# Two memory-attention and gMLP blocks: the gMLP rebuilt with tokens on partitions and started during the attention's last rows, attention weights kept on chip, the input read directly

## The chip, the cores and the metric

One core of one Trainium2 chip. The metric is the device time of one execution in microseconds (us). TensorE, its weight loads, VectorE, ScalarE, GpSimd and the issuing queue of SyncE are called PE, PEld, DVE, ACT, POOL and SP below, as in the profile.

## The reference

The input is one sequence of 2048 tokens with 512 features. Four residual steps follow each other: attention A, gMLP B, A again, B again, each on a layer norm of x, with the same weights in both rounds.

```python
x = x + A(layernorm(x));  x = x + B(layernorm(x))      # twice
# A: 64 segments of 32 tokens, one after the other; 32 heads of 128
h = concat([mem, xs])                  # 8 memory rows and 32 tokens
q, k, v = h @ Wq, h @ Wk, h @ Wv
o = softmax(mask(q @ k.T * scale)) @ v @ Wo
mem = o[:8];  out_segment = o[8:]
# B: 688 gate features
z = gelu(x @ w_in);  z1 = z[:, :688];  z2 = layernorm(z[:, 688:])
y = (z1 * (w_sp @ z2 + b_sp[:, None])) @ w_out         # w_sp: 2048 x 2048 over tokens
```

A is a chain: the memory of a segment is the output of the one before. B mixes all tokens, so its gate needs every tile of z2.

## The kernel before

**Start.** 12 MB of Wq, Wk, Wv and 4 MB of Wo are loaded on the queues of SP, ACT and POOL, in pieces of 1 MB. The input comes behind Wo on ACT's queue, 16 tiles of 128 tokens; each is cast to f32 in the permuted column order that A uses, written to the DRAM buffer `xd`, and its mean and variance are taken (`_stats`, L111 on, into `MV`). One Sqrt over all 16 tiles and a reciprocal (`_ln_scalars`, L104) then give the reciprocal deviation of every tile.

**A** (`a_block`). `ln_load` and `ln_apply` normalise a tile, write it to DRAM (`xn_d`) and read it back in two layouts (`preB`, `pre`). `b_units` projects the last eight rows of each segment of a tile (psb, L404). `segment` runs 64 times: projections of 32 rows (psm, L404), scores, softmax, values, `wo_pass` (pw, L495), which gives the next memory and so the next `hA` (L560). `spare` holds work for DVE's gaps. The output rows go to DRAM (`oA_d`, `oB_d`). `y_load` (L530 to 535) gathers a tile of them and of x with nine DMAs on SP, `y_add` adds them on DVE (L542), stores the tile to `xd` and takes its statistics. At the end come one last `wo_pass`, 32 matmuls for the last group of rows (pwB, L504), and then `y_load` and `y_add` for tile after tile through a single buffer, for the six tiles that are left.

**B** (`b_block`). First `_ln_scalars` over all 16 tiles, so every row of A must be done. Then every tile of x is loaded, normalised on DVE (L156), transposed on PE (pT, L160) and copied into `xnT` by ACT. z2 is projected with tokens on partitions (L168, L171), z1 with features on partitions (L183). The norm of z2 waits for the statistics of all tiles (L188), and then writes z2n, half the tiles on DVE (L191) and half on ACT (L194). `w_sp` comes through transposing DMAs of 256 tokens, 1 MB each, two buffers (L206); the pool of these buffers is opened when the first half is closed. The gate then has features on partitions: per 256 tokens 6 chunks of features (the last one 48 wide) by 16 token tiles of matmuls with 256 columns (pg, L223), the bias added on DVE (L226), the product with z1 on POOL (L227), and 12 matmuls with w_out (py, L234). In the first B, POOL issues the load of the attention weights for the second round at the start of this stage (`mid_hook`).

**Order.** In A, the order of PE, DVE and ACT is that of the code (`manual_schedule`); in B, the framework orders all engines. POOL and SP are ordered by the framework throughout. A queue issues its DMAs in order, and a DMA that waits holds up those behind it.

Of the kernel before, what the change touches and what calls it, by code (L numbers as in the profile page):

```python
# [26 lines left out]
FCH = [(0, 128), (128, 128), (256, 128), (384, 128), (512, 128), (640, 48)]  # L27

# [10 lines left out]
class _RR:  # L39

    def __init__(self, engines):
        self.engines = list(engines)
        self.i = 0

    def __call__(self):
        e = self.engines[self.i % len(self.engines)]
        self.i += 1
        return e


def _consts(ctx, tc):
    nc = tc.nc
    cp = ctx.enter_context(tc.tile_pool(name="consts", bufs=1))
    tctx = ExitStack()
# [42 lines left out]
    c["maskM"] = maskM  # L97
    c["MV"] = [cp.tile([P, 16, 2], F32, name=f"MV{i}") for i in range(2)]
    tctx.close()
# [4 lines left out]
def _ln_scalars(nc, pool, MV, NT, c):  # L104
    rstd = pool.tile([P, NT], F32, name="rstd")
    nc.scalar.activation(out=rstd[:], in_=MV[:, 0:NT, 1], func=ACT.Sqrt, bias=c["eps_t"][:], scale=1.0)  # L106
    nc.vector.reciprocal(out=rstd[:], in_=rstd[:])
    return MV[:, 0:NT, 0], rstd
# [8 lines left out]
def b_block(tc, c, xd, MV_in, MV_out, w_in, w_sp, b_sp, w_out, S, out_final=None, mid_hook=None):  # L117
    nc = tc.nc
    NT = S // P
    TCW = min(512, S)  # L120
    NTC = S // TCW
    TC2 = min(256, S)
    NTC2 = S // TC2
    with ExitStack() as ctx:
        mid = ctx.enter_context(tc.tile_pool(name="b_mid", bufs=1))
        ps_pool = ctx.enter_context(tc.tile_pool(name="b_ps", bufs=1, space=PSUM))
        ps = _Tagged(ps_pool, "acc", 6)
        pst = _Tagged(ps_pool, "tp", 2)
        z1T = mid.tile([P, 6, S], BF16, name="z1T")
        z2n = mid.tile([P, NT, FH], BF16, name="z2n")  # L130
        w_out_sb = mid.tile([P, 6, DM], BF16, name="w_out_sb")
        nc.scalar.dma_start(w_out_sb[:, 0:5, :], w_out[0:640, :].rearrange("(fc p) d -> p fc d", p=P))
        nc.scalar.dma_start(w_out_sb[0:48, 5, :], w_out[640:688, :])
        bsp_bc = mid.tile([P, S], BF16, name="bsp_bc")
        nc.gpsimd.dma_start(bsp_bc[:], b_sp.partition_broadcast(P))

        with ExitStack() as c1:
# [11 lines left out]
            for tt in range(NT):  # L149
                xs = xp.tile([P, DM], F32, name="xs")  # L150
                xq().dma_start(xs[:], xd[tt * P:(tt + 1) * P, :])
                xs_tiles.append(xs)
# [643 lines left out]
```

## Time and profile before

| | |
|---|---|
| median of 3 runs | 2098.46 us (2096.6 to 2102.81) |
| the profiled execution | 2104.0 us |
| its span, first to last instruction | 2102.3 us |
| busy in the span: PE, PEld, DVE, ACT, POOL | 85%, 51%, 59%, 49%, 7% |
| granted TensorE clock, mean | 0.958 |
| DMA | 144.79 MB, 69 GB/s over the span |

Matmuls are pipelined, so the time of one contains the way through the array: 96 matmuls that are called 273 ns each pass in 10.71 us. A pace is therefore read from starts, not from a mean. "Issue" is idle time for which the profile shows no wait. The view by stages gives, for stretches of the span, the busy time of each engine with the number of instructions in brackets, the granted clock and the DMA engines' busy share and rate.

### The profile page before, as it was taken

The numbers are of one execution on the slowest core, as the hardware profiler recorded it, in microseconds if no ns is written. First come the engines' busy times: TensorE is split into PE (matmuls) and PEld (weight loads), VectorE is DVE, ScalarE is ACT, GpSimd is POOL, SyncE is SP. The second block draws the span as 40 slices with busy tenths as digits, with TensorE's granted clock in tenths as the row PEclk, the third lists the DMA queues.
The fourth block names the chain that finished last, engine by engine and source line by source line (L and its number), as shares of the span: only waits on it lengthen the run. The fifth ranks groups of instructions, "written<-read, shape, count | busy, mean of one in ns | idle before, by whom it ended". The sixth has DMA issues, their size and how long they took to land.

```text
span 2102.3 us, 95923 instructions
## 1 busy us (share of the span) xinstructions
PE 1788.5 (85%) x44288; PEld 1076.1 (51%) x44288; DVE 1247.1 (59%) x2732; ACT 1024.3 (49%) x1798; POOL 138.6 (7%) x287
## 2 busy tenths in 40 slices
PE   0599999999999998273986999999999999973899
PEld 0255555555555554132753555555555555542476
DVE  1576766777777765241334676767867777644322
ACT  0366666656666664170003666656666666532500
POOL 2000000000000000001320000000000000000022
PEclk9999999999999999696998999999999999996999
DMA  9300001021002002528551000000200120044253
GB/s 355 118 24 19 21 19 27 23 68 37 20 26 79 20 15 85 168 63 253 146 172 54 23 19 27 24 20 26 79 20 20 41 71 18 10 129 130 51 141 91
DMA packets 172115, 144.79 MB, mean 69 GB/s; under 512 B 97088, under 2 KB 139712, under 8 KB 168640
## 3 DMA queue, kind: packets, MB, share of 16 engines
q1 hardware_dynamic: 146016, 83.76, 14.9%
q10 hardware_dynamic: 21728, 30.78, 4.2%
q0 software_dynamic: 3968, 24.12, 3.1%
q8 instruction: 346, 5.67, 1.1%
q14 instruction: 57, 0.47, 0.1%
HBM read 88.13 MB, written 33.70 MB: 58 GB/s over the span
## 4 chain that ended last, share of the span: by engine, by line
PE 66%; ACT 11%; DVE 9%; issue 7%; DMA 4%; SPq 1%; POOL 1%; ACTq 0%; DVEq 0%; POOLq 0%
PE psm L404 22%; PE pw L495 11%; PE psb L404 9%; PE pg L223 8%; DVE KA L588 4%; ACT rows L584 4%; ACT E L612 3%; PE psO L631 3%; PE pwB L504 3%; PE psS L608 3%; DVE E L615 2%; DMA xb<-in_A_x_dram 2%; PE psM L675 2%; PE psD L684 2%; PE py L234 1%
## 5 line engine op out<-in xcount | busy, mean ns | idle before, releaser
L404 PEld LDWEIGHTS <-hA 128*32 128x32 bf16 x12288 | 304.4, 96 | 309.1 <-DVE hA L560 54.2
L584 ACT CAST rows<-psm 128x512 bf16<-128x512 f32 x512 | 299.7, 585 | 187.4 <-PE psm L404 187.4
L495 PE MATMUL pw<-Wo_sb,uT 128*32 128x128 bf16 x16640 | 266.6, 219 | 30.5 <-issue 23.4
L404 PE MATMUL psm<-Wq_sb,hA 128*32 128x512 bf16 x4096 | 272.5, 381 | 11.7 <-DVE hA L560 11.6
L495 PEld LDWEIGHTS <-uT 128*32 128x32 bf16 x16640 | 245.2, 97 | 70.4 <-issue 31.9
L404 PE MATMUL psm<-Wk_sb,hA 128*32 128x512 bf16 x4096 | 268.5, 379 | 0.0
L404 PE MATMUL psv<-Wv_sb,hA 128*32 128x512 bf16 x4096 | 268.0, 382 | 0.0
L588 DVE STREAM_TRANSPOSE QQ<-rows 128x512 bf16<-128x512 bf16 x256 | 182.2, 712 | 81.2 <-ACT rows L584 80.7
L223 PE MATMUL pg<-wspT,z2n 128*128 128x256 bf16 (+1 forms) x1536 | 177.0, 277 | 57.1 <-issue 47.2
L647 DVE TENSOR_TENSOR uT<-psO,Rt 128x384 bf16<-128x384 f32 x256 | 138.0, 539 | 138.3 <-ACT Rt L637 138.3
L588 DVE STREAM_TRANSPOSE KA<-rows 128x512 bf16<-128x512 bf16 x256 | 182.0, 711 | 39.5 <-ACT rows L584 37.2
L223 PEld LDWEIGHTS <-z2n 128*128 128x128 bf16 (+1 forms) x1536 | 151.4, 100 | 82.5 <-issue 64.5
L612 ACT ACTIVATE E<-psS 128x448 bf16<-128x448 f32 x256 | 140.0, 547 | 107.5 <-PE psS L608 107.5
L594 DVE CAST VA<-psv 128x512 bf16<-128x512 f32 x256 | 175.4, 685 | 2.4
L226 DVE TENSOR_TENSOR gb<-pg,bsp_bc 128x256 f32<-128x256 f32 x96 | 40.6, 423 | 209.1 <-PE pg L223 209.1
L404 PEld LDWEIGHTS <-hB 128*32 128x32 bf16 x3072 | 75.4, 97 | 158.1 <-DVE hB L453 76.5
L404 PE MATMUL psb<-Wq_sb,hB 128*32 128x512 bf16 x1024 | 69.5, 393 | 100.5 <-DVE hB L453 76.5
L608 PEld LDWEIGHTS <-KA 128*64 128x64 bf16 x2048 | 79.8, 113 | 127.8 <-DVE KA L588 127.8
L553 POOL COPY QQ<-QTB 128x256 bf16<-128x256 bf16 x128 | 49.4, 401 | 1406.8 <-DVE QTB L483 795.6
L637 ACT ACTIVATE Rt<-Rt 128x1024 f32<-128x1024 f32 x128 | 135.3, 1057 | 4.1
L636 ACT ACTIVATE Rt<-psD 128x1024 f32<-128x1024 f32 x128 | 128.6, 1005 | 0.1
L106 ACT ACT_TABLE_LOAD x6 | 7.7, 1283 | 229.5 <-DMA Wo_sb<-in_A_Wo_dram 161.7
(97 smaller groups left out, 2377.5 us busy)
## 6 DMA issues: line engine op xcount, KB each, us to landing
xs<-xd SPq DMA_DIRECT2D x48, 256.0 KB
xs<-xd ACTq DMA_DIRECT2D x48, 256.0 KB
oA_d<-o_sb SPq DMA_DIRECT2D x130, 64.0 KB
xs_y<-xd SPq DMA_DIRECT2D x32, 256.0 KB
xd<-ot_y SPq DMA_DIRECT2D x32, 256.0 KB
Wq_sb<-in_A_Wq_dram POOLq DMA_DIRECT2D x6, 1024.0 KB, 16.7
Wk_sb<-in_A_Wk_dram POOLq DMA_DIRECT2D x6, 1024.0 KB, 25.0
Wv_sb<-in_A_Wv_dram POOLq DMA_DIRECT2D x6, 1024.0 KB, 20.6
```

The source lines that it names most:

```text
L223: nc.tensor.matmul(pg[0:fsz, :], lhsT=z2n[:, st_i, f0:f0 + fsz], rhs=wspT[:, st_i, :], start=(st_i == 0), stop=(st_i == NT - 1))
L404: nc.tensor.matmul(ps[32 * cg:32 * cg + 32, :], lhsT=lhs(kt, cg), rhs=rhs(kt, cg), start=(kt == 0), stop=(kt == KT - 1), tile_position=(0, ...
L495: nc.tensor.matmul(po[32 * cg:32 * cg + 32, 0:128], lhsT=lhs[:, n, :], rhs=wo_rhs(h, cg), start=(h == 0), stop=(h == H - 1), tile_position ...
L504: nc.tensor.matmul(pwB[:], lhsT=oBs[G][:, n, :], rhs=Wo_sb[:, h, :].rearrange("p (kt g el) -> p g kt el", kt=4, g=4), start=(h == heads[0] ...
L584: nc.scalar.copy(r[:], ps[:])
L588: nc.vector.transpose(out=QQ[:, j % 2, :, 0:32] if j < 2 else KA[:, j % 2], in_=r[:])
L594: nc.vector.tensor_copy(VA[:, r].rearrange("p i e -> p (i e)"), ps)
L608: nc.tensor.matmul(pS[64 * g:64 * g + 64, i, c0:80 if K is KA else 112], lhsT=K[:, r, n:n + 2, :].rearrange("p h k -> p (h k)"), rhs=q if ...
L612: nc.scalar.activation(out=E[:, r], in_=pS, func=ACT.Exp, scale=scale)
L636: nc.scalar.activation(out=o, in_=in_, func=ACT.Ln)
L637: nc.scalar.activation(out=o, in_=o, func=ACT.Exp, scale=-1.0)
L647: nc.vector.tensor_tensor(out=hview(uT_nxt, 2 * r, 2 * r + 2, 8, 32), in0=oview(2 * r, 2 * r + 2, 8, 32), in1=Rr[:, :, :, 0:24], op=ALU.mult)
```

## The change

- The input is no longer copied to `xd`. A class `_Rows` holds the handling of rows: in the first A it loads tiles of the input itself in bf16 and takes their statistics in `spare`. The reciprocal deviation of a tile is made by itself: with Ln and Exp on ACT (`_rstd_act`), or with three Newton steps, 12 small operations, on DVE (`_rstd_dve`).
- Wq, Wk, Wv are loaded once, in pieces of 0.5 MB, all on POOL's queue, and stay on chip. Wo (4 MB) is loaded again for the second A, also on POOL's queue.
- Of the last rows of A, tiles 12 to 15 are no longer added in A. Their steps are handed to B as a list `late`: while B projects tiles 0 to 5 it loads one tile, adds it on POOL, and takes its statistics on DVE.
- B works tile by tile of 128 tokens, all with tokens on partitions, and the code's order holds there too for PE, DVE and ACT. Its first stage normalises x on POOL, transposes it, projects z2 and z1 in one go (three accumulations of 512, 512 and 352 columns), takes the statistics of z2, and for every two tiles makes the deviation and z2n on DVE. The gate has `w_sp` as weights and z2n as the moving side (512 and 176 columns); the bias is a scalar per partition, so bias and product are one DVE operation from PSUM; the product is transposed on PE for w_out. `w_sp` is loaded in 16 pieces of 0.5 MB, three buffers.
- The second A's tiles 0 and 1 are normalised and sent to DRAM while B's gate goes on.

```diff
+def _rstd_act(nc, out, var, c):
+    nc.scalar.activation(out=out, in_=var, func=ACT.Ln, bias=c["eps_t"][:], scale=1.0)
+    nc.scalar.activation(out=out, in_=out, func=ACT.Exp, scale=-0.5)
+def _rstd_dve(nc, pool, out, var, n):
...
+    for k in range(3):
+        q = pool.tile([P, n], F32, name=f"nq{n}")
+        nc.vector.tensor_tensor(out=q[:], in0=y, in1=y, op=ALU.mult)
+        nc.vector.tensor_tensor(out=q[:], in0=q[:], in1=t[:], op=ALU.mult)
...
+        nc.vector.scalar_tensor_tensor(out=o, in0=q[:], scalar=1.5, in1=y, op0=ALU.add, op1=ALU.mult)
...
+    def y_add(self, tb, first, MV, eng):
...
+        eng.tensor_tensor(out=_perm(o) if first else o, in0=_perm(o) if first else o, in1=_nat(xs[:]) if first else xs[:], op=ALU.add)
+        self.nc.sync.dma_start(self.xd[tb * P:(tb + 1) * P, :], o)
+        _stats(self.nc, self.pool, o, MV[:, tb, :])
...
+        def turn_x(tt):
+            xn = zp.tile([P, DM], BF16, name="xn")
+            nc.gpsimd.tensor_scalar(out=_nat(xn[:]), in0=_perm(xt.pop(tt)[:]), scalar1=MV_in[:, tt, 0:1], scalar2=RS_in[:, tt:tt + 1],
+                                    op0=ALU.subtract, op1=ALU.mult)
...
+        def project(tt):
+            pz = big.tile([P, 1536], F32, name="pz")
+            for c0, c1 in ((0, 512), (512, 1024), (1024, FF)):
                 for kt in range(KT):
+                    nc.tensor.matmul(pz[:, c0:c1], lhsT=xnT[tt][:, kt, :], rhs=w_in_sb[:, kt, c0:c1], start=(kt == 0), stop=(kt == KT - 1))
...
+            z2[tt] = zp.tile([P, FH], F32, name="z2", bufs=3)
+            nc.scalar.activation(out=z2[tt][:], in_=pz[:, 0:FH], func=ACT.Gelu_apprx_tanh)
+            nc.scalar.activation(out=z1[:, tt, :], in_=pz[:, FH:FF], func=ACT.Gelu_apprx_tanh)
...
+        for tt in range(NT):
...
+            if tt + 1 < NT:
+                turn_x(tt + 1)
+            project(tt)
+            if late:
+                late.pop(0)()
+            if tt % 2 == 1:
+                _rstd_dve(nc, zp, RSz[:, tt - 1:tt + 1], MVz[:, tt - 1:tt + 1, 1], 2)
+                normalise(tt - 1)
+                normalise(tt)
...
+        def product(t):
...
+                load_wsp(t + 3)
+            u[t] = gp.tile([P, FH], BF16, name="u")
+            nc.vector.scalar_tensor_tensor(out=u[t][:], in0=pg.pop(t)[:, 0:FH], scalar=c["bsp"][:, t:t + 1], in1=z1[:, t, :],
+                                           op0=ALU.add, op1=ALU.mult)
...
+        for t in range(NT):
+            gate(t, range(0, 4))
+            if t > 0:
+                turn_u(t - 1)
+            gate(t, range(4, 12))
+            if t > 0:
+                finish(t - 1)
+            gate(t, range(12, NT))
+            product(t)
...
+    for k, r in ((0, 0), (1, 0), (0, 1), (1, 1), (2, 0), (2, 1)):
...
+            nc.gpsimd.dma_start(w[k][:, kt, 2048 * r:2048 * r + 2048], srcv[:, kt, 2048 * r:2048 * r + 2048])
...
+    def step(tb):
+        if tb > NB - 4:
+            rows.y_add(tb - 1, first, MV_out, nc.gpsimd)
+        if tb < NB:
+            rows.y_load(tb, first)
+
+    return [lambda tb=tb: step(tb) for tb in range(NB - 4, NB + 1)] + [late_rstd]
```

In `finish`, the w_out matmuls (py) are followed on DVE by the sum with x and, in the first B, by the statistics of the new rows, and `_rstd_act` on ACT; for tiles 0 and 1 the next A's normalisation comes too.

How the instructions stand. On POOL, at the start of the program, before: Wq_sb and the others are the attention weights, uT is A's output tile.

```order
L83 AFFINE_SELECT maskf<-maskf 32x4x8 x2
L355 DMA Wq_sb<-in_A_Wq_dram 128x4096
L355 DMA Wk_sb<-in_A_Wk_dram 128x4096 x2
L355 DMA Wv_sb<-in_A_Wv_dram 128x4096 x2
L388 DMA Wo_sb<-in_A_Wo_dram 128x8x512 x2
L413 MEMSET uT_320 128x1024
```

And now, at the same place (bsp is the gate's bias, one number per token):

```order
L92 DMA bsp_bf<-in_B_b_sp_dram 128x16x1
L73 AFFINE_SELECT maskf<-maskf 32x4x8 x2
L407 DMA Wq_sb<-in_A_Wq_dram 128x2048 x2
L93 CAST bsp<-bsp_bf 128x16
L407 DMA Wq_sb<-in_A_Wq_dram 128x2048 x2
L407 DMA Wk_sb<-in_A_Wk_dram 128x2048 x4
L407 DMA Wq_sb<-in_A_Wq_dram 128x2048 x4
L407 DMA Wk_sb<-in_A_Wk_dram 128x2048 x4
L407 DMA Wv_sb<-in_A_Wv_dram 128x2048 x8
L436 DMA Wo_sb<-in_A_Wo_dram 128x8x512 x4
```

All weights stand in one queue, in the order in which `b_units` uses them, and from the third piece on they stand behind a cast that waits for the bias's load. The first two input tiles on SP lie where the bias lay before, so they wait for that cast too.

On DVE, where B begins, before: the last two of A's rows (ot_y), the one reciprocal, the normalisation of x and the first statistics of z.

```order
L542 TENSOR_TENSOR ot_y<-ot_y,xs_y 128x512
L113 BN_STATS bnst<-ot_y 128x6
L114 BN_AGGR MV_115<-bnst 128x2
L107 RECIPROCAL rstd<-rstd 128x16
L156 TENSOR_SCALAR xn<-xs,MV_115,rstd 128x512 x11
L176 BN_STATS bnst_25667<-z_25653 128x6
```

And now, after the last row that A itself adds (y_o is a tile of A's rows, nt and nq belong to the Newton steps, of which some are left out between the pieces here):

```order
L244 BN_AGGR MVz<-bnst_25492 128x2
L130 BN_STATS bnst<-y_o 128x6
L131 BN_AGGR MV_116<-bnst 128x2
L114 TENSOR_SCALAR nt_25512<-MVz 128x2
L116 TENSOR_SCALAR nb_25514<-nt_25512 128x2
```

```order
L124 SCALAR_TENSOR_TENSOR RSz<-nq_25527,ny_25525 128x2
L247 TENSOR_SCALAR z2n<-z_25447,MVz,RSz 128x688
L247 TENSOR_SCALAR z2n<-z_25489,MVz,RSz 128x688
L242 BN_STATS bnst_25560<-z_25557 128x6
L243 BN_STATS bnst_25560<-z_25557 128x6
L244 BN_AGGR MVz<-bnst_25560 128x2
L130 BN_STATS bnst<-y_o 128x6
```

The normalisation of x has left DVE. The statistics of a late row tile, which POOL adds after SP has loaded it, now stand in DVE's order between the statistics of z2 and the normalisation of the first two z2 tiles; the next late tile stands one projected tile further on, and so on for four.

On PE, in the gate, before: the end of the last chunk of features (48 of them) against 256 tokens, where such a pair comes 16 times for a chunk, and the first two of the 12 matmuls with w_out.

```order
L223 LDWEIGHTS z2n
L223 MATMUL pg<-wspT,z2n 48x256
L223 LDWEIGHTS z2n
L223 MATMUL pg<-wspT,z2n 48x256
L234 LDWEIGHTS uT
L234 MATMUL py<-w_out_sb,uT 128x512
L234 LDWEIGHTS uT
L234 MATMUL py<-w_out_sb,uT 128x512
```

And now, around the transposes of the tile before:

```order
L280 LDWEIGHTS wspT
L280 MATMUL pg<-z2n,wspT 128x512
L280 LDWEIGHTS wspT
L280 MATMUL pg<-z2n,wspT 128x176
L294 LDWEIGHTS u
L294 MATMUL pT<-ident_bf,u 128x128
```

The moving side has 688 columns per pair of token tiles, in two matmuls with the same weights, and six transposes stand four of sixteen steps into the next tile's gate.

More of the change, by code (lines that the diff above doesn't have):

```diff
@@ L336 @@
+    for blk in range(2):
+        late = a_block(tc, c, rows, MV[0], RS[0], MV[1], RS[1], wqkv, A_Wo, S, first=(blk == 0))
+        b_block(tc, c, rows, xd, MV[1], RS[1], MV[0], RS[0], B_w_in, B_w_sp, B_w_out, S, late, out_final=out2 if blk == 1 else None)
 class _Tagged:
@@ L556, in build_hA @@
         def build_hA(s, pw):
-            t = pre.pop(s)
+            t = rows.pre.pop(s)
             if pw is not None:
@@ L711, in segment @@
                 prep_segment(s + 1)
-        for tb in range(2):
-            ln_load(tb)
-            ln_apply(tb)
         ln_turn(0)
@@ L730, in a_block @@
                 if tb + 2 < NB:
-                    ln_load(tb + 2)
+                    rows.load(tb + 2, first, nc.sync)
             def spare():
```

442 lines of the change are left out of this document (190 added, 252 removed).

## The prediction

> **What bounds the kernel now.** The view by stages comes first, cut where the chain of waits changes hands: start, A, its last projections (pwB), B's row sums, projections, the wait ahead of the gate, the gate, `b_units`; then the second round.
>
> ```profile
> core 0: us, PE busy (x) PEld busy (x) DVE busy (x) ACT busy (x) POOL busy (x), PEclk, DMA share, GB/s
> 0.00:84.00 84.00, 7.47 (x100) 3.08 (x104) 24.58 (x70) 5.80 (x8) 15.07 (x48) 1.00 0.81 293
> 84.00:838.10 754.10, 719.11 (x20865) 423.00 (x20860) 532.55 (x1153) 455.64 (x795) 23.58 (x61) 1.00 0.12 34
> 838.10:847.10 9.00, 8.95 (x35) 3.50 (x32) 1.57 (x3) 0.28 (x2) 0.00 (x0) 0.79 0.70 219
> 847.10:887.40 40.30, 1.53 (x13) 1.17 (x14) 10.10 (x20) 3.24 (x5) 0.56 (x1) 0.56 0.37 119
> 887.40:934.80 47.40, 44.53 (x278) 23.98 (x276) 27.10 (x70) 42.22 (x82) 0.70 (x2) 0.98 0.17 60
> 934.80:980.40 45.60, 0.03 (x1) 0.06 (x2) 0.00 (x0) 0.00 (x0) 5.59 (x11) 0.53 1.06 314
> 980.40:1093.80 113.40, 112.32 (x864) 83.56 (x864) 41.42 (x91) 0.00 (x0) 33.89 (x50) 0.98 0.50 131
> 1093.80:1125.10 31.30, 7.32 (x101) 3.31 (x104) 7.50 (x16) 5.80 (x8) 2.94 (x6) 0.62 0.59 192
> 1125.10:1878.40 753.30, 718.89 (x20868) 421.88 (x20864) 532.20 (x1153) 455.73 (x795) 23.62 (x61) 1.00 0.12 34
> 1878.40:1887.80 9.40, 9.37 (x35) 3.60 (x32) 1.57 (x3) 0.27 (x1) 0.00 (x0) 0.75 0.65 207
> 1887.80:1930.00 42.20, 3.52 (x23) 2.40 (x24) 11.31 (x23) 4.54 (x8) 0.56 (x1) 0.52 0.42 129
> 1930.00:1983.80 53.80, 42.76 (x266) 22.84 (x264) 25.89 (x68) 40.92 (x80) 0.00 (x0) 0.94 0.28 73
> 1983.80:2102.30 118.50, 112.66 (x864) 83.73 (x864) 31.36 (x64) 9.88 (x16) 32.06 (x48) 0.98 0.44 110
> ```
>
> In A and in the gate PE is full. The change hardly touches A's matmuls, so A stays. PE stands idle, at a low clock, in the start (76 us), in the row sums (39 and 39), ahead of the first gate (46) and after it (24). There the change can win. The chain of waits shows what those stretches wait for.
>
> ```profile
> 9.55 36.63 DMA xb<-in_A_x_dram
> 830.62 3.19 issue
> 836.26 1.57 issue
> 860.57 2.00 DMA xd<-ot_y
> 867.62 2.08 DMA xd<-ot_y
> 908.88 0.86 PE pz2a L168 x4
> 910.05 0.86 PE pz2a L168 x4
> 934.78 45.59 issue
> 980.37 13.17 PE pg L223 x96
> 1024.55 10.71 PE pg L223 x96
> 1038.46 10.71 PE pg L223 x96
> 1117.80 7.36 PE psb L404 x92
> ```
>
> The start waits for x, which stands behind 16 MB of weights. The row sums go through one buffer, a tile per 7.05 us (867.62 − 860.57, from store to store). The 45.59 us called "issue" are a DMA wait: two stretches of the stage view, the first inside it and the second in the second round, show why.
>
> ```profile
> 945.00:970.00 25.00, 0.00 (x0) 0.00 (x0) 0.00 (x0) 0.00 (x0) 2.11 (x4) 0.50 1.02 412
> 1975.00:1984.00 9.00, 0.15 (x1) 0.14 (x2) 0.00 (x0) 0.48 (x1) 0.00 (x0) 0.70 1.06 203
> 828.50:834.00 5.50, 2.14 (x139) 1.97 (x142) 3.12 (x9) 1.68 (x2) 0.00 (x0) 1.00 1.01 328
> ```
>
> With the weights for round two in flight the engines move 412 GB/s and `w_sp` comes last; without them its first two pieces take about 9 us at 203 GB/s. In the third row, at the end of A, tiles of x are loaded in advance.
>
> **The change part by part.** The profiled execution took 2104.0 us, 5.5 above the median of 2098.46; its span is 2102.3, with 1.7 around it. The sum is made on the span.
>
> *Start, 84.0 to 50.* POOL's constants end near 9.5, where the chain begins. A cast that waits for the bias follows two pieces of Wq; a load on POOL's queue landed in 7.5 us at the median, so the cast is done near 17. Behind it stand 22 pieces, 11.5 MB; at 412 GB/s that is 28 us. The last Wv lands at 45; the first `b_units` eat Wq, Wk, Wv as they land, x passes beside them, and first psm comes at 47, with 3 for a cold clock. If the cast hides nothing it is 44. Before, x came after Wo; now Wo is last, and needed 10 us after psm.
>
> ```profile
> bsp_bc<-in_B_b_sp_dram POOLq DMA_DIRECT2D x2, 512.0 KB, 7.5
> L542 DVE TENSOR_TENSOR ot_y<-ot_y,xs_y 128x512 f32<-128x512 f32 x32 | 22.1, 690 | 83.5 <-DMA ot_y<-oB_d 74.4 <-DMA oA_d<-o_sb 9.0
> L113 DVE BATCH_NORM_STATS2 bnst<-ot_y 128x6 f32<-128x512 f32 x32 | 22.2, 695 | 1.1
> L176 DVE BATCH_NORM_STATS2 bnst<-z 128x6 f32<-128x344 f32 x32 | 16.2, 505 | 0.8 <-ACT z L173 0.8
> L177 DVE BATCH_NORM_STATS2 bnst<-z 128x6 f32<-128x344 f32 x32 | 15.6, 488 | 0.4 <-ACT z L174 0.4
> L178 DVE BATCH_NORM_AGGREGATE MVz<-bnst 128x2 f32<-128x12 f32 x32 | 6.4, 201 | 0.6
> L188 DVE SCALAR_TENSOR_TENSOR nmrz<-MVz,rstd 128x16 f32<-128x16 f32 x2 | 0.3, 175 | 0.1
> L191 DVE TENSOR_SCALAR z2n<-z,MVz,rstd 128x688 bf16<-128x688 f32 x16 | 8.9, 633 | 0.0
> L227 POOL TENSOR_TENSOR uT<-gb,z1T 128x256 bf16<-128x256 f32 x96 | 64.2, 668 | 238.3 <-DVE gb L226 238.3
> L238 DVE TENSOR_TENSOR xo<-py,xs 128x512 f32<-128x512 f32 x32 | 22.0, 690 | 28.4 <-PE py L234 27.9
> ```
>
> *A, 763.1 to 757.5 (first) and 762.7 to 756 (second).* Tiles of x no longer load in A's last microseconds, so the issue gaps there (3.19 and 1.57) go, and pwB comes at full clock, 2 us less: −7. First A gains statistics of 14 tiles and single deviations; DVE is busy 532 of 754, so they cost 1.3; should none fit a gap, 14 × 1.6 us is 20 or so. By "Runtime: NRT & Kernel Launch", section "Instruction fetch mechanics", of the Trainium skill, instruction fetch is streamed and mostly hidden, so the gap in a straight program should not be there at all; the row's DMA share of 1.01 with 3.19 idle beside it says that it isn't hidden when the engines are full. Were the gaps another thing, as they would be by that rule, the sum would be 10 higher.
>
> *B's first stage, to the first gate tile: 75.* Before: 40.3 + 47.4 + 45.6 = 133 in the first B, 96 in the second. Now projection starts with tile 0 while A's rows are summed, but POOL adds a late tile in 1.34 (two of 668) where DVE took 0.69, so the single buffer turns in 7.05 + 0.65 = 7.7. Tile 11 is summed 6 us after A, tile 12 near 17 (SP's queue also holds three transposing loads of w_sp ahead, 13 to 22), and tile 15 near 41. The statistics of tile 12 stand in DVE's order ahead of the first norm of z2, and z2 has three buffers, so projection waits for the chain: it goes with the late tiles. By 47 the deviations of the last rows and the first pair are made (12 small operations of 0.175, twice) and two pairs are through. The other pairs cost DVE 2 × (0.505 + 0.488 + 0.201) + 12 × 0.175 + 2 × 0.633 = 5.8, against PE's 2 × 2.3 (5,504 columns at 1.17 per 2,752): 5 × 5.4 = 27, first gate tile at 75. The pre-gate wait of 46 goes: no weights but Wo are loaded, and w_sp's pieces come with the late rows.
>
> *Gate, 13.91 per 256 tokens to 13.2 and 14.0.* Before, 96 pg of 256 columns took 10.71, and 12 py with the gaps the rest, 3.2. Now a tile of 128 tokens takes 16 × 688 columns: at 1.17 per 4 × 688 that is 4.67; 6 transposes of 128 columns 0.33, 6 py with gaps 1.6: 6.6. DVE's xo, statistics and product (0.69 + 0.69 + 0.18 + 0.78) fit, but the first two stand ahead of the product, so 0.4 is lost in the first B: 7.0. 15 tiles: 105 and 99. After the last tile come 4.5 to `b_units` in the first B (no more 24: two tiles of x are normalised during the gate, 2 us for it) and 7 to the end in the second.
>
> *First B* is then 75 + 105 + 2 + 4.5 = 186.5 against 270.7 (847.1 to 1117.8); *second B* 75 + 99 + 7 = 181 against 214.5. `b_units` keeps 7.4. Wo, loaded beside PE's first segments twice, may slow them: +5 by choice, 0 to 10.
>
> The sum: 50 + 757.5 + 186.5 + 7.4 + 756 + 181 + 5 = 1943.4 of span, 1945.1 of run; less 5.5 to stand with the median, **1940 us**.
>
> **The rivals.** *The weights go one after another* (0.08). 412 GB/s was seen with pieces of 1 MB queued; now 0.5 MB. Were each paced by its own landing, 1.27 of data and 1.4 of a landing (the store of a row tile, 2.00, less the time of its own 256 KB), 24 × 2.7 is 65: start at 81, time 1971. For it: POOL issues only so many at once. Against: the row with 412. "DMA: Bandwidth & Descriptors", section "Bandwidth", of the Trainium skill asks for 1 MiB or more per transfer; by its rule each piece would cost more, 24 × 3.2 = 77 by the fit that the skill gives, and the time would be about 1983 (an estimate).
>
> ```profile
> wspT<-in_B_w_sp_dram SPq DMA_TRANSPOSE x16
> ```
>
> *The late rows hide* (0.10): the deviations come when projection needs them, B's first stages are 55 to 65 and the time is 1920 down to 1905. For it: projection of 12 tiles is 28 us of PE. Against: the order of DVE.
>
> *DVE sets the gate* (0.12). If the product waits for finish's sums, a tile is 8.6 instead of 6.8: 30 × 1.8 = +54, 1994. Against: DVE's work per tile is 2.4 of 6.6.
>
> *w_sp's loads set the gate: the slower side* (0.04). There are 16 pieces of 0.5 MB, where there were 8 of 1 MB, in each B. The forecast wins 158, so 32 tiles may lose 4.9 each; it is slower once a half piece takes over 6.8 + 4.9 = 11.7 us. For it: the 2 MB ahead of the gate took 45.6 while weights came, 11.4 for 0.5 MB. With 12 per tile it is 32 × 5.2 = 166 more: 2106. Against: 2 MB in 9 us at 203 GB/s, and the weights no longer come.
>
> **How the numbers follow.** My forecast has 0.62; the rest (0.04) is spread. The range is to hold 8 in 10: the start's 44 to 75, the late chain's ±9 twice and A's bound give 1905 to 1990 for the forecast with the first two rivals in it; the gate on DVE and the slower side lie outside. Against a bound of 0.3%, 6 us, about what a measurement tells from no change, every case but the last is faster: 0.94, same 0.02, slower 0.04.
>
> **What would show it.** After: first psm near 50 and the DMA share at 1.0 ahead of it; the row sums' pace 7.7 with POOL as adder; first pg 75 after the end of pwB, with pw's issue gaps gone; gate tiles 6.6 to 7 apart, py beside them. The prediction is wrong where pg starts are 8 or more apart, where the wait before psm is as long as the weights one by one, or where the first pg comes with the projections, before the last rows' statistics.

## The result and the profile after

The changed kernel takes 2018.88 us (median of 4 runs, 2014.49 to 2021.39) against 2100.26 before on the same chip: a ratio of 0.9612, 95% interval 0.9588 to 0.9635. It is faster by half of what was forecast (1940), and lies above the range.

The view by stages of the profiled execution (span 2016.6), cut at the first psm, the end of pwB, the first pg, the first psb of round two and its first psm, and so on:

```profile
core 0: us, PE busy (x) PEld busy (x) DVE busy (x) ACT busy (x) POOL busy (x), PEclk, DMA share, GB/s
0.00:49.40 49.40, 8.12 (x97) 3.05 (x101) 8.09 (x25) 5.20 (x10) 27.16 (x69) 0.99 0.79 292
49.40:816.60 767.20, 729.42 (x20900) 429.55 (x20892) 544.78 (x1184) 466.21 (x844) 26.32 (x64) 1.00 0.12 33
816.60:911.40 94.80, 52.07 (x251) 25.04 (x257) 44.45 (x164) 36.99 (x56) 39.85 (x22) 0.78 0.38 107
911.40:1031.60 120.20, 109.91 (x696) 57.58 (x709) 44.16 (x87) 23.65 (x65) 1.00 (x2) 1.00 0.52 135
1031.60:1036.90 5.30, 5.30 (x100) 2.68 (x104) 3.63 (x7) 3.31 (x7) 3.57 (x4) 1.00 0.24 74
1036.90:1805.20 768.30, 729.99 (x20900) 426.59 (x20896) 535.06 (x1156) 460.53 (x817) 27.96 (x68) 1.00 0.13 38
1805.20:1900.80 95.60, 54.08 (x252) 25.84 (x258) 44.34 (x163) 36.98 (x56) 41.06 (x22) 0.79 0.43 114
1900.80:2016.60 115.80, 107.76 (x691) 57.55 (x703) 31.52 (x53) 14.90 (x34) 0.00 (x0) 0.99 0.46 114
```

Against the terms of the sum (the gate's first tile, 7.0 and 6.6, is taken out of the 75; Wo's 5 is split over both A):

| stage | before | forecast | after |
|---|---|---|---|
| start to first psm | 83.9 | 50 | 49.4 |
| first A, to the end of pwB | 763.2 | 760 | 767.2 |
| first B, to the first pg | 133.3 | 68 | 94.8 |
| first pg to `b_units` | 137.4 | 118.5 | 120.2 |
| `b_units` | 7.2 | 7.4 | 5.3 |
| second A | 762.7 | 758.5 | 768.3 |
| second B, to the first pg | 96.1 | 68 | 95.6 |
| first pg to the end | 118.4 | 113 | 115.8 |

The miss is 73 us of span: 27 and 28 stand in the two first stages of B, 17 in the two A, 5 in the gates, and 3 came back in the start and `b_units`. The first stage of the second B, rebuilt from end to end, takes as long as the old one with its row sums: 95.6 against 96.1. No engine is full there (PE 54 of 96, DVE 44, ACT 37, POOL 41) and the DMA engines are at 0.43, so it is a chain that hands over from engine to engine. A piece of the chain of waits, late in the first B's stage, shows the hands. Its first row is the norm of the third pair of z2 tiles, which comes behind the statistics of the last late row:

```profile
879.72 0.65 DVE z2n L247
...
880.56 2.54 DMA xs<-xd
...
883.29 2.10 POOL xn L224
...
885.45 0.61 PE pT L228 x4
886.05 2.99 PE pz L236 x7
...
893.60 2.85 DMA xs<-xd
```

A tile of x is loaded, normalised on POOL, transposed and projected, and the next load that matters starts only after a projection. The group of the normalisation and POOL's waits, in that stage and in the whole span, say what this costs:

```profile
L224 POOL TENSOR_SCALAR xn<-xs,MV,RS 128x512 bf16<-128x512 f32 x32 | 68.4, 2140 | 105.8 <-DMA xs<-xd 99.4 <-PE pz L236 5.7 <-PE pT L228 0.6
```

```profile
POOL xn L224 <- DMA xs<-xd: 46.3, 11, 9.8
PE pT L228 <- POOL xn L224: 42.2, 11, 8.9
ACT z L239 <- DVE z2n L247: 18.1, 2, 9.2
```

PE waits 42 us for POOL, and POOL 46 for x. The third row is another chain: ACT, which also issues the loads of x, waits for a buffer of z2, which DVE frees only after the late rows' statistics.

### The profile page after: what moved, and what is told of

It reads as the page before. It is cut to its first block, busy times and chain, and to the rows that moved or that the text cites. A ratio compares the mean times of both kernels' runs of the same rounds, so it can differ in the third digit from the quotient of the medians.

```text
span 2016.6 us, 95153 instructions
## 1 busy us (share of the span) xinstructions
PE 1796.6 (89%) x43866; PEld 1027.9 (51%) x43904; DVE 1256.0 (62%) x2835; ACT 1047.8 (52%) x1888; POOL 166.9 (8%) x249
## 4 chain that ended last, share of the span: by engine, by line
PE 63%; DVE 12%; ACT 10%; DMA 6%; issue 4%; POOL 2%; SPq 1%; DVEq 0%; POOLq 0%; ACTq 0%
PE psm L452 22%; PE pw L509 10%; PE psb L452 8%; PE pg L280 5%; DVE KA L588 5%; ACT rows L584 4%; ACT E L612 3%; PE psO L631 3%; PE psS L608 3%; DVE E L615 3%; PE pwB L518 2%; PE py L303 2%; PE pz L236 2%; DMA xs<-xd 2%; PE psM L675 2%
## 5 line engine op out<-in xcount | busy, mean ns | idle before, releaser
L452 PEld LDWEIGHTS <-hA 128*32 128x32 bf16 x12288 | 308.5, 96 | 307.9 <-DVE hA L560 47.1
L452 PE MATMUL psm<-Wq_sb,hA 128*32 128x512 bf16 x4096 | 275.3, 384 | 11.3 <-DVE hA L560 10.8
L280 PE MATMUL pg<-z2n,wspT 128*128 128x176 bf16 (+1 forms) x1002 | 158.9, 308 | 4.0 <-DVE z2n L247 2.2
L608 PEld LDWEIGHTS <-KA 128*64 128x64 bf16 x2048 | 79.7, 113 | 127.8 <-DVE KA L588 127.4
L692 DVE TENSOR_TENSOR uT<-psO,Rm 128x128 bf16<-128x128 f32 x256 | 62.7, 286 | 92.5 <-PE psO L631 92.4
L608 PE MATMUL psS<-QQ,KA 128*64 128x80 bf16 x2048 | 109.9, 208 | 10.2
L280 PEld LDWEIGHTS <-wspT 128*128 128x128 bf16 x1024 | 85.4, 98 | 65.1 <-issue 9.8
L615 DVE TENSOR_TENSOR E<-E,maskN 128x448 bf16<-128x448 bf16 x256 | 95.0, 371 | 31.4 <-ACT E L612 31.4
```

Source lines behind the costliest of these rows:

```text
L280: nc.tensor.matmul(pg[t][:, c0:c1], lhsT=wsp[t][:, st, :], rhs=z2n[:, st, c0:c1], start=(st == 0), stop=(st == NT - 1))
L452: nc.tensor.matmul(ps[32 * cg:32 * cg + 32, :], lhsT=lhs(kt, cg), rhs=rhs(kt, cg), start=(kt == 0), stop=(kt == KT - 1), tile_position=(0, ...
L608: nc.tensor.matmul(pS[64 * g:64 * g + 64, i, c0:80 if K is KA else 112], lhsT=K[:, r, n:n + 2, :].rearrange("p h k -> p (h k)"), rhs=q if ...
L615: nc.vector.tensor_tensor(out=E[:, r], in0=E[:, r], in1=maskN[:, j4, :].unsqueeze(1).to_broadcast([P, 4, 112]), op=ALU.mult)
```

## The experiments

Each kernel was timed in three rounds beside the kernel before; ratios are to it, with 95% intervals. The stages come from each run's profiled execution, cut as above.

| run | median us | ratio | first stage of B, first and second, us |
|---|---|---|---|
| changed kernel | 2018.88 | 0.9612 (0.9588 to 0.9635) | 94.8, 95.6 |
| e1_xn_dve | 2127.98 | 1.0133 (1.0115 to 1.0152) | 145.9, 149.5 |
| e2_x_ahead | 2021.98 | 0.9623 (0.9602 to 0.9644) | 86.5, 96.2 |
| e3_late_first | 2051.01 | 0.9764 (0.9735 to 0.9793) | 106.9, 116.2 |
| e4_weights_again | 2057.68 | 0.9788 (0.9769 to 0.9807) | 121.1, 99.7 |
| e5_wsp_late | 2021.58 | 0.9623 (0.9608 to 0.9637) | 96.1, 99.3 |
| e6_late_dve | 2015.35 | 0.9579 (0.9553 to 0.9605) | 90.4, 101.3 |
| e7_no_late | 1998.86 | 0.9509 (0.9490 to 0.9527) | 85.6, 87.6 |
| e8_both | 2011.91 | 0.9576 (0.9561 to 0.9590) | 91.8, 91.3 |
| e9_order | 2010.11 | 0.9567 (0.9552 to 0.9582) | 90.0, 90.3 |
| e10_order_no_late | 1974.01 | 0.9409 (0.9390 to 0.9428) | 67.9, 77.0 |
| e11_ahead_no_late | 1964.87 | 0.9354 (0.9338 to 0.9370) | 65.2, 67.7 |
| e12_order_both | 1989.42 | 0.9473 (0.9459 to 0.9488) | 81.1, 81.1 |
| e13_rstd_once | 2031.77 | 0.9675 (0.9634 to 0.9716) | 99.7, 108.2 |
| e14_before_nkq2 | 2100.3 | 1.0000 (0.9980 to 1.0021) | 133.3, 95.6 |
| e15_all | 1986.93 | 0.9470 (0.9437 to 0.9503) | 79.7, 83.3 |

### x normalised on DVE

```diff
-            nc.gpsimd.tensor_scalar(out=_nat(xn[:]), in0=_perm(xt.pop(tt)[:]), scalar1=MV_in[:, tt, 0:1], scalar2=RS_in[:, tt:tt + 1],
+            nc.vector.tensor_scalar(out=_nat(xn[:]), in0=_perm(xt.pop(tt)[:]), scalar1=MV_in[:, tt, 0:1], scalar2=RS_in[:, tt:tt + 1],
                                     op0=ALU.subtract, op1=ALU.mult)
```

> The changed kernel with x normalised on DVE in B's first stage, as the kernel before did. Theory one (POOL's 2.07 us per tile, in line with a load of x that ACT issues only behind the gelu of the tile before, sets the first stage, and the late sums on POOL queue behind it): DVE takes 0.54 per tile, the late sums come every 7.7 us instead of 10.6, the later tiles every 3.5 instead of 3.9; each B gains 12 to 18 us, the kernel comes to 1983 to 1995. Rival one (the late rows' own loads and stores set the stage): gain under 5 us in all, 2014 to 2019. Rival two (the loads of x set the pace, whoever normalises): 5 to 10 us in all.

Measured 2127.98: 109 us slower, the worst of all, though the operation itself takes a quarter (0.54 against 2.07). The chain of waits of this run, two tiles of it:

```profile
879.45 0.75 ACT z L239
880.23 0.52 DVE bnst L242
...
886.19 0.63 DVE z2n L247
886.82 0.47 DVE xn L224
887.33 0.61 PE pT L228 x4
887.94 4.60 PE pz L236 x12
892.57 0.75 ACT z L239
```

DVE works in the order of the code. There the normalisation of a tile stands behind the statistics and norm of the one before, so gelu, statistics, norm, next normalisation, transposes and projection follow each other with nothing beside them; PE waits, and the projection takes 4.60, at a granted clock of 0.50 in that stretch (887.3 to 892.5 us), instead of 2.34 to 2.50. Theory one was wrong: POOL is slow, but as a queue of its own it lets x run ahead.

### x loaded four tiles ahead

```diff
-            xt[tt] = gp.tile([P, DM], F32, name="xs")
+            xt[tt] = gp.tile([P, DM], F32, name="xs", bufs=4)
-            if tt + 2 < NT:
-                load_x(tt + 2)
+            if tt + 4 < NT:
+                load_x(tt + 4)
```

and two buffers of `w_sp` instead of three.

> The changed kernel with four buffers for x in B instead of two, so that tiles of x are loaded four ahead; w_sp has two buffers instead of three to make room. x is still normalised on POOL. Theory one: POOL's 2.07 us stays, the 2.5 to 3.8 us of the load leaves the chain; 5 to 10 us per B, 1999 to 2009. Rival one (late rows): nothing, 2014 to 2022. Rival two (loads of x): 12 us or more per B, 1995 or less, and then more than the normalisation on DVE gives.

Measured 2021.98, no gain; the first B's stage is 8 shorter, the second's not, and the gates are 6.5 and 4 longer. ACT's timeline shows what took the load's place:

```profile
865.87 0.74 ACT L239 ACTIVATE z<-pz 128x688 f32<-128x688 f32 x1 [15.80 <-DVE z2n L247]
...
883.01 0.74 ACT L239 ACTIVATE z<-pz 128x688 f32<-128x688 f32 x1 [13.52 <-DVE z2n L247]
```

The projections run ahead until the three z2 buffers are full, and then wait for the late rows. By itself this fits rival one; what the load ahead did gain in both B is seen further down, where the stage is cut at the last late sum.

### The late rows ahead of the projections

```diff
+        while late:
+            late.pop(0)()
         load_x(0)
```

> The changed kernel with the steps of the last four row tiles all ahead of B's first projection instead of between the projections of tiles 0 to 4. Theory one: the late sums then do not stand behind POOL's normalisation and turn in 7.7 us, 38 us in all; 16 tiles of projection follow at 3.9, 62 us; first gate matmul 100 to 105 us after A against 95 and 102, 0 to +12 us in all. Rival one (the row chain is the same wherever it stands, and the projections really hide it): 57 us of rows and 62 of projections, +24 per B, 2065.

Measured 2051.01: the stages grow by 12 and 21. Interleaving is worth that much, between what the two theories gave.

### The weights loaded again

```diff
         if out_final is None:
             _ln_exp_table(nc)
+            mid_hook()
```

Here `mid_hook` issues the 24 loads of Wq, Wk and Wv on POOL's queue.

> The changed kernel with Wq, Wk, Wv loaded again on POOL's queue at the start of the first B's gate, as the kernel before did with all four. My account of the saved wait (45.6 us ahead of the first gate) says that most of the first B's gain is the absence of this traffic: w_sp's pieces come slower while 12 MB pass, 30 us at 412 GB/s; three pieces are already there and cover 21 us, so the loss is 10 to 30 us, 2029 to 2049. Rival: three pieces in hand and 0.5 MB per tile hide it, under 5 us, and the old wait was the pool of w_sp opening late, not the weights.

Measured 2057.68, 38.8 us slower where 10 to 30 were expected, and not in the gate, which stays at 121.5. POOL's timeline shows that the framework put the loads ahead, from A's last segment into the first stage:

```profile
796.95 2.14 POOL L414 DMA_DIRECT2D Wq_sb<-in_A_Wq_dram  x4 [17.15 <-PE psm L458]
...
863.04 1.12 POOL L414 DMA_DIRECT2D Wv_sb<-in_A_Wv_dram  x2
```

First A grows by 8 and the first stage by 26, beside the 12 MB. So 39 us is what keeping these weights on chip is worth here; the old kernel paid 46 at another place.

### The loads of w_sp held back, the late rows on DVE

The first edit is to take SP's delay away: in the changed kernel SP issues three transposing loads ahead of tile 12's, and the first two hold it for 8 us. SP's timeline there:

```profile
822.05 8.03 SPq L220 DMA_TRANSPOSE wspT<-in_B_w_sp_dram  x2
```

```diff
             wsp[t] = wsp_pool.tile([P, NT, P], BF16, name="wspT")
+            if t < 3:
+                nc.vector.memset(wsp[t][:, 0, 0:1], 0.0)
...
-        for t in range(3):
-            load_wsp(t)
...
             if late:
                 late.pop(0)()
+            if tt == 4:
+                for t in range(3):
+                    load_wsp(t)
```

> The changed kernel with the first three loads of w_sp held back until the last late tile has its statistics (DVE writes one element per partition of their buffers after those, so that the loads wait for it). In the changed kernel SP issues them ahead of tile 12's loads and is held 10.5 us by them. Theory two (the chain of late rows sets the first stage, and what stands ahead of its steps in SP's and POOL's queues lengthens it): tile 12 is summed 8 to 10 us sooner, first gate matmul 6 to 10 us sooner in each B, 1999 to 2007. Rival (the ring of z2 buffers, ACT's load of x and POOL's normalisation sets the stage by itself): under 4 us in all. In both, should the first gate tiles then wait for w_sp, some of it is given back.

> The changed kernel with the late rows summed on DVE instead of POOL. On POOL the sums of tiles 13 and 15 stood behind normalisations whose x had not landed (2 and 5 us). Theory two: they no longer do, 5 to 8 us less per B, 2003 to 2009. Rival (an engine that works in order must not be given a step that waits for a load, as with the normalisation on DVE, which cost 109 us): DVE holds the statistics of z2 and the norms behind the row's load, 10 us or more per B slower, 2040 or more.

The second edit is one word, `nc.gpsimd` to `nc.vector` in the late `y_add`. The third run has both.

> The loads of w_sp held back and the late rows summed on DVE, both edits together. Theory two: the late chain turns in 7 to 8 us from 7 us after A on, 37 instead of 56 us; first gate matmul 12 to 18 us sooner in each B, 1983 to 1995. Rival as for the sums on DVE alone: no better than w_sp held back alone.

Measured 2021.58, 2015.35 and 2011.91. Held back alone nothing is gained, but that run did not make the chain shorter: the last late sum came 55.0 us after A in the first B and 57.5 in the second, against 55.8 and 56.0 in the changed kernel. SP, free of the loads of w_sp, issued tile 12's rows in the first B only 4.5 us sooner (12.8 us after A instead of 17.4), because it then waited for the store of tile 11 to leave the one buffer of row tiles; and POOL's sum stood behind a normalisation whose x was still on its way, so that it came 2 us sooner (22.1 instead of 24.0). On DVE alone the intervals tell nothing apart: the last late sum came 5 us sooner in the first B and 6 later in the second, and the stages went with it (90.4 and 101.3). With both edits the last late sum came 6 us sooner in each B, and the kernel gained 7 us, at the edge of what the intervals tell apart, of the 24 to 36 that theory two gave.

### Without the late rows

```diff
-        self.nc.sync.dma_start(self.xd[tb * P:(tb + 1) * P, :], o)
-        _stats(self.nc, self.pool, o, MV[:, tb, :])
+        for q in (tb,) if tb < 11 else range(11, 16):
+            self.nc.sync.dma_start(self.xd[q * P:(q + 1) * P, :], o)
+            _stats(self.nc, self.pool, o, MV[:, q, :])
...
-    return [lambda tb=tb: step(tb) for tb in range(NB - 4, NB + 1)] + [late_rstd]
+    return [late_rstd]
```

> The changed kernel without the sums of the last four row tiles: tile 11's sum and its statistics are stored in their places too, so the rows of tiles 12 to 15 are left out of the computation. The first stage then has only x, POOL's normalisation, the projections and the norms of z2. Theory two: 16 tiles at 3.8 to 3.9, the pace of the last tiles in the changed kernel, and the first load, 65 to 72 us to the first gate matmul instead of 95: 1965 to 1976. Rival (the stage is bound by its own ring, the late rows are hidden in it): 85 us or more, 1998 or more.

This kernel leaves the sums of tiles 12 to 15 out, as the later ones named `no_late` do. Measured 1998.86, with 85.6 and 87.6 in the stages: the rival. What is left without late rows is plain in the chain of waits of this run:

```profile
867.46 2.55 DMA xs<-xd
...
870.21 2.07 POOL xn L225
...
872.33 0.40 PE pT L229 x4
872.73 4.02 PE pz L237 x12
...
876.83 2.54 DMA xs<-xd
...
879.55 2.08 POOL xn L225
...
881.68 0.40 PE pT L229 x4
882.08 2.34 PE pz L237 x12
...
884.50 2.59 DMA xs<-xd
```

From load to load it is 9.4 and 7.7 us, for two tiles each. ACT issues the load of tile t+2 behind the gelu of tile t−1; on PE, the transposes of t+2 stand ahead of the projection of t+1; so that projection waits for POOL, the next load waits for its gelu, and the ring is closed. PE idles 2.4 of each turn by its timeline, and in some turns its clock falls: the granted clock is 0.61 from 872.33 to 876.75 us, where the projection takes 4.02, and 1.00 from 881.68 to 884.42, where it takes 2.34.

```profile
872.33 0.40 PE L229 MATMUL pT<-ident_bf,xn 128*128 128x128 bf16 x4 [2.44 <-POOL xn L225]
881.68 0.40 PE L229 MATMUL pT<-ident_bf,xn 128*128 128x128 bf16 x4 [2.40 <-POOL xn L225]
```

### Opening the ring

```diff
             nc.scalar.copy(xnT[tt][:].rearrange("p kt r -> p (kt r)"), pT[:, 0:512])
+            if tt + 2 < NT:
+                load_x(tt + 2)
...
             del xnT[tt]
+            if tt + 1 < NT:
+                turn_x(tt + 1)
             z2[tt] = zp.tile([P, FH], F32, name="z2", bufs=3)
...
-            if tt + 2 < NT:
-                load_x(tt + 2)
-            if tt + 1 < NT:
-                turn_x(tt + 1)
             project(tt)
```

The next tile's transposes now stand between a projection's matmuls and its gelus.

> The changed kernel with another order in B's first stage: the transposes of the next tile stand behind the projection of this one on PE (they stood ahead of it), its copy on ACT ahead of this tile's gelus, and the load of x two tiles on right behind that copy. Theory three (a ring sets the stage: gelu of a tile, load of x two tiles on, POOL's normalisation, its transposes, the projection behind them on PE, its gelu; 2.6 + 2.1 + 0.6 + 2.4 to 4.5 + 0.7, some 9 us for two tiles, 4.4 to 4.7 each): now a projection no longer waits for the normalisation of the next tile, and the pace falls towards DVE's 3.5 per tile; without late rows in the way 14 us less, with them 6 to 14 less per B: 1991 to 2007. Rival (the late rows' chain and the ring have the same length, so that each hides the other): under 6 us in all.

> The order of the run before (transposes behind the projection, the load of x behind the copy), and the sums of the last four row tiles left out (tile 11's sum stands in their places). Theory three: nothing but x, POOL, PE and DVE is left, and DVE's 3.5 us per tile sets the pace: 62 to 70 us from A's end to the first gate matmul in each B, against 86 and 88 with the old order; 1959 to 1975. Rival (POOL's normalisation and the load, 4.7 us per tile one after the other, set the pace in any order): 80 us or more, 1985 or more.

> The old order, x loaded four tiles ahead (four buffers of x, two of w_sp), and the sums of the last four row tiles left out. Theory three: the 2.6 us of the load leave the ring of two tiles, 9 to 6.5 us, or DVE's 7: 64 to 72 us from A's end to the first gate matmul, 1968 to 1982 (the gate loses some 4 per B with two buffers of w_sp, as it did before). Rival (the load was never in the ring; with late rows loading ahead gave nothing): 84 us or more, 1998 or more.

> All rows computed: the new order of the first stage, the late rows summed on DVE, and the loads of w_sp held back behind them. Theory three: the ring no longer sets the stage, so now the late chain does, and shortening it pays, other than with the old order (1 to 4 us per B): 20 to 28 us less per B, 1963 to 1980. Rival (late rows hidden in the ring before and after): no better than the new order alone.

Measured 2010.11 for the order alone (stages 5 shorter, total 9 lower, just short of what was expected); 1974.01 without late rows (68 and 77, the second above the 62 to 70 expected: in its first tiles a load of x took 6.5 us); 1964.87 with the old order, x ahead and without late rows (65 and 68, somewhat better than expected); 1989.42 for the order with the shorter late chain and all rows computed, 14 less per B where 20 to 28 were expected.

Removing the late rows alone gives 9 and 8 us, the load ahead alone 8 and −1, both together 30 and 28. So two chains share the stage, and the timelines of POOL and DVE show where one hands over to the other. In us, from the end of pwB to the last late sum (tile 15), and from there to the first pg:

| run | first B | second B |
|---|---|---|
| forecast | 41 + 27 | 41 + 27 |
| changed kernel | 55.8 + 39.1 | 56.0 + 39.6 |
| e4_weights_again | 81.2 + 39.9 | 60.0 + 39.7 |
| e5_wsp_late | 55.0 + 41.1 | 57.5 + 41.8 |
| e6_late_dve | 50.5 + 39.9 | 61.6 + 39.7 |
| e8_both | 49.9 + 41.9 | 50.0 + 41.3 |
| e2_x_ahead | 56.3 + 30.2 | 66.1 + 30.1 |
| e9_order | 54.9 + 35.1 | 54.6 + 35.7 |
| e12_order_both | 46.7 + 34.4 | 46.7 + 34.4 |

Up to the last late sum the late chain sets the time, because the three z2 buffers stop the projections; the two are still tied together there, as POOL's sums stand behind its normalisations. Behind it the remaining pairs go at the pace of the ring: 39 to 42 us with the old order, whatever was done to the late rows; 34 to 36 with the new order; 30 with x ahead. The load ahead thus took 9 us out of the second part in both B; in the second B the late sums came 10 us later, and the gain was lost. Without late rows the ring sets all sixteen tiles and takes 86 by itself, so that their removal alone shows little.

In the chain of waits of the last run, late in its stage, a tile takes 3.45 us, and nothing but PE and one copy is left in the ring: the projection, the next tile's transposes, and ACT's copy of them, for which PE sits idle 0.73 us a tile by its timeline.

```profile
881.44 2.50 PE pz L240 x12
883.94 0.24 PE pT L230 x4
...
884.25 0.59 ACT xnT L232
...
884.89 2.50 PE pz L240 x12
```

This version beats both kernels, by 5.3% and by 1.5% (1989.42 / 2018.88).

### A's segments

```diff
         def y_add(tb):
             rows.y_add(tb, first, MV_out, nc.vector)
-            copies.append(lambda: _rstd_act(nc, RS_out[:, tb:tb + 1], MV_out[:, tb, 1:2], c))
...
+        for q in range(0, NB - 8, 4):
+            _rstd_dve(nc, rows.pool, RS_out[:, q:q + 4], MV_out[:, q:q + 4, 1], 4)
         for tb in ys + due:
...
+        _rstd_dve(nc, rows.pool, RS_out[:, NB - 8:NB - 4], MV_out[:, NB - 8:NB - 4, 1], 4)
```

> The changed kernel with the deviations of A's summed tiles 0 to 11 made at the end of A in three small runs of Newton steps on DVE, instead of tile by tile with Ln and Exp on ACT inside A. Theory four (the single deviations, 10 a round on ACT in A's order, lengthen the segments from 11.70 to 11.78 us, and in B's first tiles their tables alternate with gelu's, 4 loads of 1.28 us): both A blocks 4 to 6 us shorter, and the first stages 0 to 4, 2003 to 2011. Rival (the segments' spread has another cause; Wo's late landing and the cold clock of the first segment are the whole of it): 2014 to 2020.

> The kernel before with one edit: two buffers of QQ instead of three, as the changed kernel has. If the third buffer gave POOL's copies room, each segment grows by some 0.08 us, 128 of them 10 us: 2108 to 2113. If not: within 3 us of the kernel before, as I assumed.

> The new order of the first stage, the late rows summed on DVE, w_sp held back, and the deviations of tiles 0 to 11 on DVE at the end of A. Theory four: 6 to 14 us less than without the last edit (1989), 1975 to 1983. Rival: 1986 to 1992.

Measured 2031.77, 2100.3 and 1986.93. Theory four falls: first A is 767.7 without the single deviations, as with them (second A, 763.1, lies in the spread of the other runs, 762.2 to 768.3), and the segments of the first, from the second on, keep a mean of 11.80 us (11.78 in the changed kernel, 11.70 before). The run is 13 slower by its median, at the edge of what the intervals tell apart; in its profiled execution, the slowest of the four, both first stages grew, by 5 and 13, and the first gate by 7, with 36 small operations of DVE at the joint in each A; that these are the cause is argued. With the new order they cost nothing that the intervals tell (1986.93 against 1989.42). Two buffers of QQ instead of three change nothing.

## Why the prediction was wrong

**The start came out right**: 50 forecast, 49.4 measured. The first psm follows the last piece of Wv, as forecast; PE's timeline has the psb that waited for it:

```profile
49.01 0.62 PE L452 MATMUL psb<-Wv_sb,hB 128*32 128x512 bf16 x4 [0.86 <-DMA Wv_sb<-in_A_Wv_dram]
```

That the number is so near is partly luck: the cast was done at 13.4 instead of 17, the 22 pieces behind it took 36 us to the last landing at 49.0 instead of 28, and of the 5 for the rest of `b_units` and a cold clock 0.4 came. The pieces of 0.5 MB do not cost what the rival of weights one by one had, 2.7 us each: the last four of Wv release their psb 1.4 us apart (44.86, 46.23, 47.75 and 49.01), and between 14 and 44 us the view by stages has the core at 384 GB/s. POOL does hold each piece back until the eighth before it has landed, which was the argument for that rival, but at these rates it costs nothing that the row shows. The Trainium skill, "DMA: Bandwidth & Descriptors", section "Bandwidth", asks for 1 MiB or more per transfer; the 3.2 us per piece that the prediction worked out by it did not come either.

```profile
14.00:44.00 30.00, 6.54 (x80) 2.59 (x80) 5.59 (x12) 3.43 (x9) 14.23 (x26) 1.00 1.01 384
```

**The gate was right**: 7.0 and 6.6 per tile forecast, 7.01 and 6.76 measured, by the starts of the last 16 pg of a tile in the chain of waits of the first and the second B; only the first three tiles of the first B took 8.2 to 8.4, 3.7 us more in all where 2 were forecast. The loads of w_sp did not set it. In the first B the chain does run through DVE, whose sum with x and statistics stand ahead of the product:

```profile
951.04 2.44 PE pg L280 x16
...
954.91 0.70 DVE xo L312
...
956.55 0.83 DVE u L287
...
958.05 2.44 PE pg L280 x16
```

```profile
1960.12 2.44 PE pg L280 x16
1966.88 2.44 PE pg L280 x16
```

That is the 0.4 that the forecast gave it, and it came out as 0.25 a tile; the rival in which DVE sets the gate had 1.8.

**The step that failed is "B's first stage, to the first gate tile: 75"**, which came out at 102 (94.8 and a tile of 7.0). It had two parts: the late rows' chain up to 47, then five pairs at 5.4 by DVE's and PE's work. That the projections wait for the late rows was right. By the table above, the last late sum came at 56 us instead of 41, and from there to the first pg it took 39 instead of 27: 15 and 12 of the 27 us.

The first part was mis-sized: POOL's adds took 1.15 to 1.26, near the 1.34 taken, but tile 12 was summed 24 us after A, where I took 17 out of 13 to 22, and the sums then came 10.6 us apart instead of 7.7, since POOL's order had tiles 13 and 15 behind normalisations, for the last of which x was still on its way. POOL's timeline has the first and the last of the four adds:

```profile
840.54 1.16 POOL L181 TENSOR_TENSOR y_o<-y_o,y_xb 128x512 f32<-128x512 f32 x1 [1.29 <-DVE MVz L244]
...
868.24 4.13 POOL L224 TENSOR_SCALAR xn<-xs,MV,RS 128x512 bf16<-128x512 f32 x2 [7.08 <-DMA xs<-xd]
872.33 1.15 POOL L181 TENSOR_TENSOR y_o<-y_o,y_xb 128x512 f32<-128x512 f32 x1
```

The second part was wrong in kind. I compared the engines' work per tile and took the pace from it, 5.4 a pair (DVE's own sum, in the same sentence, is 5.8, and would have added 2 us); POOL's normalisation had no term at all, and the order that ties ACT's load of x to a gelu, and PE's projection to the next tile's transposes, I had read and not followed around. By DVE's timeline the norms of the last pairs came 7.2 us apart in the first B. With x loaded ahead they came 5.8 apart, DVE's own sum: the pace that I forecast holds once the ring is open. Without late rows the ring alone gives 86; without the ring's load, and without late rows, the stage is 65 to 68, which is what I forecast with both in it. The rivals missed it too: "the late rows hide" was given 55 to 65 us, as if nothing else were there.

Of POOL's 2.07 us per tile the trace of before had no row; the two nearest, DVE's 0.54 and POOL's product at 1.34 per 512 columns, are both too low. The Trainium skill, "GPSIMD Engine Reference", section 4.1 "Engine selection", has one-input operations on that engine at roughly line rate; this one, f32 to bf16 with a permuted order, takes 3.8 times DVE's time. The measurement decides.

**The 46-us wait ahead of the gate did go.** With the weights loaded again 39 us come back, but elsewhere: 25 of them in the late chain of the first B, whose last sum came at 81 us instead of 56. So the price is of the traffic beside a chain of transfers, not of the gate. That the old kernel's wait was this traffic fits its 412 GB/s there and the 9 us of its second B without it; no run took the traffic out of the old kernel.

**A was forecast 3 and 4 us shorter and came out 4 and 6 longer.** (The forecast of the table has Wo's 5 in it.) Of the 7 us that I took off the end of A, 4.2 and 4.9 came: from the first psm of the last segment to the end of pwB it is 22.5 and 22.9 us, against 26.7 and 27.8 (24.8 and 26.8 in the old kernel with two buffers of QQ). In the first A pwB went at a granted clock of 1.00 (7.1 us) instead of 0.79 (9.0), as forecast. The issue gaps at the end of pw, which I had go with the loads of x, went only in part: from 4.8 to 3.0 us in the first A, from 5.8 to 1.6 in the second. Where they stayed, the DMA engines are at 0.34 by the view by stages (803 to 810 us), so full DMA engines are not what all of them need. PE's timeline at the end of the first A:

```profile
805.31 1.97 PE L509 MATMUL pw<-Wo_sb,uT 128*32 128x128 bf16 x128 [0.99 <-issue]
809.33 0.23 PE L509 MATMUL pw<-Wo_sb,uT 128*32 128x128 bf16 x1 [2.05 <-issue]
```

The Trainium skill, "Runtime: NRT & Kernel Launch", section "Instruction fetch mechanics", has instruction fetch mostly hidden; by that the gaps would be another thing and stay, and the sum would be 10 higher. Gaps that went in part fit neither that nor my account by itself; what they are isn't shown by any run.

The rest is in the segments. First A's first segment is 3 us longer (14.3 from its first psm to the next, 11.3 before), at a granted clock of 0.81 where it was 1.00. From the third segment on, a segment takes 11.79 us on the mean against 11.70 in the first A, and 11.75 against 11.66 in the second: 5 to 6 us in each A. The other runs of the changed kernel show it too, with 0.04 to 0.12 us a segment over the old kernel, with or without the single deviations on ACT. The statistics of the input tiles, which only the first A has, can't be the whole of it; the cause stays open. In second A the first pw waits for Wo, loaded again only after B; the chain of waits has it, and the first segment is 3 longer for it, as is the second by 1.5.

```profile
1036.91 13.68 DMA Wo_sb<-in_A_Wo_dram
```

Over the runs of the changed kernel and its variants second A lay between 762.2 and 768.3, so some of its 6 us isn't settled.

## What to carry to other kernels

When a stage is rebuilt as a pipeline, don't price it by its busiest engine: write down, for one tile, who issues its load and behind what, which engine's order puts the next tile's step ahead of this one's, and walk round until you are back; the length of that ring over the tiles in it is the pace, whatever the engines' shares are. Where two chains share a stage, undoing one of them can show little of what undoing both gives (9 or 8 us here, against 30): find the moment at which one hands over to the other, read each run's stage on both sides of it, and test the two together before saying of one that it doesn't matter. An edit that is to shorten a chain has to be checked on the chain itself: one run here moved a load away and left the chain as long as it was. A slow engine with a queue of its own can beat a fast one on which the step must wait its turn.

## What the runs showed of the hardware

POOL takes 2.07 us for a normalisation of 128x512, f32 to bf16, that takes DVE 0.54, but only 1.15 to 1.26 for a sum of two 128x512 tiles that takes DVE 0.69. Transposing loads of 0.5 MB held SP's queue for 1.9 to 3.3 us each (a median of 2.51), but the second of each B for 5.5 and 7.0; those of 1 MB before held it for a median of 4.39. The projection's 12 matmuls took 4.02 and 4.60 us where the granted clock was 0.61 and 0.50, and 2.34 at 1.00; an idle stretch of 2.4 us on PE stood ahead of a slow one and of a fast one alike. POOL issued a weight piece of 0.5 MB only once the eighth before it had landed, about every 1.4 us.
